# A gated mix of a long convolution and a token-shift MLP: keys and values channel by token instead of token by channel, and who does the small operations

## The chip, the cores and the metric

One core of one Trainium2 chip. The time is device microseconds of one launch, the median over runs; the profile is one further execution, recorded by the hardware profiler. Both kernels compute the same function in bf16 with sums in float32.

## The reference, cut to what matters

S is 2048 tokens, D 640 channels, F 1536.

```
k_shift[s] = sum over t in 0..3 of k[s - 3 + t] * shift_k[:, 3 - t]   # zeros ahead of the first token
kv  = k_shift * v
y   = irfft(rfft(kv padded to 2S) * rfft(ssm_k padded to 2S))[:S] + kv * ssm_D
a   = q * y
h   = gelu(layernorm(q) @ w1)                 # four channel groups, shifted by +1, -1, +2, -2 tokens
x1  = q + shifted(h) @ w2
b   = x1 + gelu(layernorm(x1) @ w3) @ w4
g   = sigmoid(sum over channels of q * gate_w)
out = g * a + (1 - g) * b
```

So there is a causal convolution of every channel of kv over all 2048 tokens with a filter of its own, and an MLP of two layers, mixed by one gate for each token.

## The kernel before, in words

**How order comes about.** The program is first recorded: `P.op` and `P.dma` note each operation with the memory it reads and writes, and from the memory follow the dependencies. A literal list SEQUENCE then gives the order in which the recorded operations are issued, and PLACES the PSUM bank of each matmul result; each engine gets its operations in that order and the semaphores between engines are put in where a dependency crosses. An engine never overtakes: whatever stands behind a waiting instruction in its list waits too. All SBUF tiles lie in one array (`arena`) and all PSUM tiles in another (`PSall`), so the profile tells them apart by shape and line only. Helpers hold the lines: `tt` (L636, two operands), `ts` (L641, one operand and scalars), `act` (L646, ACT), `mm` (L656, matmuls), `P.dma` (L238 plain, L235 as a DMA transpose).

**The convolution.** It is done blockwise in the frequency domain. Tokens are cut into 4 blocks of 512; a block's transform has 1024 points, of which the symmetries leave four groups `j` of 128 frequencies with a real and an imaginary part. A block is first *folded*: sums and differences of its halves, one of them reversed in time, so that each group of frequencies needs a matmul against only 128 or 256 rows. HF holds the filter's spectrum, XF that of kv, both as 2 halves of 320 channels x 4 blocks x (4 groups x 2 parts x 320).

- `h_load`, `h_fold`, `h_chunk` (L729 to 764), for each of 5 chunks of 128 channels: the filter lies channel by token, 128 x 2048. ACT reverses (4 x 255), two DVE operations of 1024 make the sum and the difference, two DMA transposes of 256 KB bring tokens onto the partitions, then 20 matmuls of 512 columns and four to eight evictions.
- `kv_half`, `kv_block` (L768 to 800), for each half of the channels g, block b and half block: k is loaded token by channel, 128 partitions x 5 neighbouring tokens x 320 channels (400 KB; the overlap serves the shift), v as 2 x 320 (160 KB). One DVE product of 2560 multiplies the 4 taps at once against the table SHK, in which the tap weights stand on all partitions; sums of 1280 and 640 add the taps; a product of 640 multiplies with v. A matmul with `flip` reverses one half block in time, ACT evicts it, and four DVE operations of 640 fold the block. For the first block a memset (L778) and three small loads stand in for the tokens ahead of the first.
- `x_fwd` (L802): 12 matmuls of 320 columns and four evictions of 640 for each g and b.
- `combine` (sums and differences of neighbouring blocks' spectra), `unit` (products of the spectra, 2560 wide, with accumulating DMAs issued by POOL for some of the sums), `final` (inverse transform, product with q, output).

**The MLP.** `ln_bn`/`bn_math`/`ln1`, `mm1` (whose token shifts are the operations of L891), `mmg` and `gate`, `mm2`, `ln2` with `ln_math`, `mm3`, `mm4`. Their statistics of 128 x 1 go over POOL (GpSimd) in good part: the power of -1/2 (`pool_pow`, L828) always, and small products and sums by the argument `eng="pool"`. POOL also issues the accumulating DMAs.

**Where it lies in time.** The MLP's first layer, the filter, the keys and values and the forward transforms share the first 119 us or so, `unit` and the MLP's second layer follow, and the inverse ends it.

Of the kernel before, what the change touches and what calls it, by code (L numbers as in the profile page):

```python
# [382 lines left out]
def _folded_dft():  # L383
# [5 lines left out]
    k = np.concatenate([np.arange(0, 256, 2), np.arange(1, 256, 2)])[None, :]  # L389
    ko = np.arange(256)[None, :]  # L390
    n = 2. * np.arange(128)[:, None] + .5
    m = 256 - n
    R = np.concatenate([np.cos(w * 2 * k * n), -np.sin(w * np.where(k == 0, 512, 2 * k) * n),
                        np.cos(w * (2 * ko + 1) * n), -np.cos(w * (2 * ko + 1) * m),
                        -np.sin(w * (2 * ko + 1) * n), -np.sin(w * (2 * ko + 1) * m)], 1)
    p = np.arange(128)[:, None]
    no = np.stack([p, p + 128])
    ne = np.where(no == 0, 256, no)
    Rh = np.stack([np.cos(w * 2 * k * ne),
                   np.where(k == 0, no == 0, -np.sin(w * 2 * k * no)),  # L400
                   np.cos(w * (2 * ko + 1) * no),
                   -np.sin(w * (2 * ko + 1) * ne)])
    Z = np.zeros((3, 128, 128))
    Z[:2, :, 0] = ((-1.) ** ne)[:, :, 0]
    Z[2, 0] = 1.
# [6 lines left out]
    Rh = Rh.transpose(2, 0, 1, 3)  # L412
    G = G.reshape(2, 2, 2, 128, 256).transpose(3, 0, 2, 1, 4)
    return (R, np.concatenate([Rh.reshape(128, 2048), Z.transpose(1, 0, 2).reshape(128, 384)], 1),
            G.reshape(128, 8 * 256))


def bass_gated_mix__ssm_conv_h3__mixer_s_mlp__prompt_kernel(
# [11 lines left out]
    cE = nc.inline_tensor(_bits(np.repeat(np.eye(5), 128, axis=1)), name="cE")  # L430

# [20 lines left out]
    def ps(n, cls):  # L452
# [3 lines left out]
    SEQUENCE = [57, 10, 31, 58, 28, 9, 11, 5, 56, 1, 27, 4, 7, 12, 0, 2, 59, 29, 13, 141, 30, 14, 63, 26, 35, 15, 64,  # L456
# [74 lines left out]

    HW = S + 4
    oXF = alloc(20480)
# [618 lines left out]
```

## Time and profile before

| | |
|---|---|
| runs | median 239.17 us, 237.65 to 246.24, 3 runs |
| profiled execution | span 236.6 us |
| matmuls of 320 columns, of 512 columns (L656) | 824, 390 |
| DVE instructions, POOL instructions | 402, 122 |
| moved by DMA | 45.48 MB in 63785 packets |

Engines in the profile: PE the matmuls, PEld their weight loads (beside PE), DVE the vector engine, ACT the scalar engine, POOL GpSimd, SP the engine that issues most DMAs. A group of instructions reads: line, engine, operation, output and input shape (partitions x elements), count, then busy time in us and the mean ns of one, then idle time of the engine just before them and what ended it. A row of waits reads: who waited, for what, total us, times, longest.

### The profile page before, as it was taken

To read this page: it belongs to the slowest core of one execution; us is meant where nothing else is said; L and a number is where in the kernel's file an instruction comes from. 1 tells how busy PE (TensorE), PEld (TensorE's weight loads), DVE (VectorE), ACT (ScalarE), POOL (GpSimd) and SP (SyncE) were. 2 spreads that over 40 slices of the span, in tenths; PEclk is the share of its full clock that TensorE was granted. 3 is DMA by queue.
4 is the path that set the end of the run, shared out by engine and by line. 5 is a ranking of instruction groups with operands and counts; after the bars stand their busy time and mean duration, and the time that the engine had idled before them with its cause. 6 is when DMAs were issued, how large, how long until landed. Compare 5 with 4: busy or idle time off the path is not lost.

```text
span 236.6 us, 4135 instructions
## 1 busy us (share of the span) xinstructions
PE 222.6 (94%) x1501; PEld 134.7 (57%) x1501; DVE 220.1 (93%) x402; ACT 171.2 (72%) x317; POOL 108.4 (46%) x122
## 2 busy tenths in 40 slices
PE   7999999999899999998989999899999999999861
PEld 2688755456444556444755457555677545776640
DVE  6889999899898789998899999999999999999975
ACT  2699889687588858998477763778968479258962
POOL 0330405810796008056109994564315256266960
PEclk9999999999999999999999999999999999999996
DMA  6999699996889999799527928869899978999996
GB/s 172 334 355 326 123 259 235 278 244 130 188 143 196 236 259 235 181 361 212 150 60 125 157 37 212 141 105 209 204 316 210 200 124 136 185 157 108 113 155 122
DMA packets 63785, 45.48 MB, mean 192 GB/s; under 512 B 28818, under 2 KB 59028, under 8 KB 63764
## 3 DMA queue, kind: packets, MB, share of 16 engines
q1 hardware_dynamic: 54748, 33.33, 56.5%
q0 software_dynamic: 8832, 11.80, 33.5%
q8 instruction: 12, 0.20, 0.3%
q10 hardware_dynamic: 184, 0.08, 0.1%
q14 instruction: 9, 0.07, 0.1%
HBM read 24.22 MB, written 6.55 MB: 130 GB/s over the span
## 4 chain that ended last, share of the span: by engine, by line
PE 30%; DMA 23%; DVE 20%; POOL 12%; issue 6%; SPq 4%; ACT 3%; DVEq 0%; POOLq 0%; ACTq 0%
PE PSall L656 27%; DVE arena L636 14%; DMA arena<-arena 8%; DMA arena<-in_A_v_dram 8%; DMA out_dram<-arena 6%; POOL out_dram L238 4%; ACT arena L646 3%; POOL arena L641 3%; PE PSall L682 3%; SPq L238 2%; POOL arena L828 2%; SPq L235 2%; DVE arena L641 2%; DVE arena L891 2%; DVE arena L824 1%
## 5 line engine op out<-in xcount | busy, mean ns | idle before, releaser
L656 PE MATMUL PSall<-arena 128*128 128x320 bf16 (+5 forms) x1444 | 214.9, 308 | 8.7 <-DVE arena L636 4.9
L636 DVE TENSOR_TENSOR arena<-arena 128x640 bf16<-128x640 bf16 (+5 forms) x247 | 183.0, 792 | 6.3 <-DMA arena<-in_A_v_dram 2.6
L656 PEld LDWEIGHTS PSall<-arena 128*128 128x128 bf16 (+1 forms) x1444 | 130.6, 98 | 92.0 <-DVE arena L636 7.4
L646 ACT ACTIVATE arena<-PSall 128x640 bf16<-128x640 f32 (+6 forms) x189 | 109.1, 632 | 34.9 <-PE PSall L656 33.5
L641 POOL TENSOR_SCALAR arena<-arena 128x1 f32<-128x1 f32 (+2 forms) x41 | 32.9, 811 | 44.2 <-DVE arena L825 22.6
L646 ACT ACTIVATE arena<-arena 128x640 bf16<-128x640 bf16 (+4 forms) x62 | 42.2, 701 | 6.9 <-POOL arena L636 3.8
L828 POOL TENSOR_TENSOR arena<-arena 128x1 f32<-128x1 f32 (+1 forms) x26 | 26.1, 1009 | 27.1 <-DVE arena L641 26.5
L238 POOL DMA_DIRECT2D out_dram<-arena x28 | 31.5, 1304 | 11.9 <-ACT arena L646 9.2
L238 POOL DMA_DIRECT2D arena<-arena x12 | 15.6, 1303 | 38.8 <-DVE arena L636 38.6
L646 ACT ACTIVATE arena<-PSall,arena 128x640 bf16<-128x640 f32 (+1 forms) x32 | 20.5, 658 | 17.6 <-PE PSall L656 16.1
L641 DVE TENSOR_SCALAR arena<-arena 128x640 bf16<-128x640 bf16 (+2 forms) x49 | 14.4, 306 | 2.9 <-DMA arena<-arena 1.4
L824 DVE BATCH_NORM_STATS2 arena<-arena 128x6 f32<-128x320 bf16 x32 | 14.2, 476 | 1.5 <-DMA arena<-in_A_q_dram 1.5
L682 PE MATMUL PSall<-arena 128*128 128x512 bf16 x15 | 6.1, 593 | 1.6 <-DVE arena L678 1.6
L636 POOL TENSOR_TENSOR arena<-arena 128x1 f32<-128x1 f32 (+1 forms) x11 | 7.2, 658 | 0.6
L926 DVE SCALAR_TENSOR_TENSOR arena<-PSall,arena 128x640 bf16<-128x640 f32 x8 | 6.5, 818 | 0.2 <-PE PSall L656 0.2
L891 DVE TENSOR_SCALAR arena<-arena 32x256 bf16<-32x256 bf16 (+1 forms) x24 | 5.7, 243 | 0.8 <-ACT arena L646 0.4
L646 ACT ACTIVATE PSall<-PSall 128x640 f32<-128x640 f32 x8 | 5.6, 701 | 0.1
L682 PEld LDWEIGHTS PSall<-arena 128*128 128x128 bf16 x15 | 2.0, 142 | 5.1 <-issue 3.5
L870 PE MATMUL PSall<-arena 128*128 128x128 bf16 x40 | 3.4, 220 | 0.0
L685 ACT ACT_TABLE_LOAD x1 | 1.3, 1283 | 2.7 <-issue 2.7
L825 DVE BATCH_NORM_AGGREGATE arena<-arena 128x2 f32<-128x12 f32 x16 | 3.0, 195 | 0.0
L870 PEld LDWEIGHTS PSall<-arena 128*128 128x128 bf16 x40 | 2.4, 98 | 0.7 <-DVE arena L825 0.2
(24 smaller groups left out, 9.3 us busy)
## 6 DMA issues: line engine op xcount, KB each, us to landing
arena<-arena POOLq DMA_DIRECT2D x12, 640.0 KB, 6.2
arena<-in_A_k_dram SPq DMA_DIRECT2D x14, 400.0 KB, 4.6
arena<-in_A_q_dram SPq DMA_DIRECT2D x14, 320.0 KB, 5.8
out_dram<-arena POOLq DMA_DIRECT2D x20, 160.0 KB, 4.9
arena<-in_A_ssm_k_dram SPq DMA_DIRECT2D x5, 512.0 KB, 6.0
arena<-in_A_v_dram SPq DMA_DIRECT2D x16, 160.0 KB, 4.3
arena<-in_B_w_dram SPq DMA_DIRECT2D x1, 1920.0 KB, 9.9
out_dram<-arena SPq DMA_DIRECT2D x10, 160.0 KB, 4.4
```

What stands on the lines that cost most here:

```text
L235: fn = lambda e: e.dma_start_transpose(out, in_)
L238: fn = lambda e: e.dma_start(out, in_, **kw)
L636: P.op(eng, lambda e: e.tensor_tensor(o, real(a), real(b), op), [a, b], [o], dve_ns(o, [a, b], 2) if eng == "dve" else 500)
L641: P.op(eng, lambda e: e.tensor_scalar(o, real(a), s1, s2, op0=op0, **({} if op1 is None else {"op1": op1})), [a] + aps, [o], dve_ns(o, [a] ...
L646: P.op("act", lambda e: e.activation(real(o), real(a), f, bias=bias, scale=scale, **({"accum_out": accum} if accum is not None else {})), ...
L656: fns.append(lambda e, l=l, r=r, i=i: e.matmul(real(o), l, r, start=(i == 0), stop=(i == last)))
L682: P.op("pe", lambda e: e.matmul(real(pw), warm[:, 0:128], warm[:, 128:640], start=True, stop=True), [warm], [pw], 427.0 if i < 14 else 216.0)
L824: P.op("dve", lambda e, o=o, i=i: e.bn_stats(o, i), [i], [o], 400)
L828: P.op("pool", lambda g: g.tensor_tensor(o, a, e, ALU.pow), [a, e], [o], dur)
L870: P.op("pe", [lambda e, c=c, pb=pb, xn=xn: e.transpose(real(pb)[:, 128 * c:128 * (c + 1)], xn[:, 128 * c:128 * (c + 1)], ident) for c in r ...
L891: P.op("dve", lambda e, o=hT[q, 4, c0:c0 + n], i=hx[q, :]: e.tensor_scalar(o, i, 1.0, None, op0=ALU.mult), [hx[q, :]], [hT[q, 4, c0:c0 + n ...
L926: P.op("dve", lambda e: e.scalar_tensor_tensor(x, real(pr), 1.0, x, op0=ALU.mult, op1=ALU.add, accum_out=st[1, 0][:, t:t + 1]), [pr, x], [ ...
```

## The change

- **Keys and values** are loaded by DMA transposes straight out of DRAM: 128 channels x 2048 tokens, 512 KB each, one of k and one of v for each of 5 chunks (`kv_load`). The shift by a token is then an offset along the row: `kv_taps` makes four operations of one operand with a weight for each channel (`taps`), three sums and one product with v, all 2048 wide. `kv_fold` does both folds in this layout (four DVE operations of 1024 and one reversal of 1024 on ACT), then one transpose of 512 KB (16 x 128) brings the folded tokens onto the partitions. `x_chunk` transforms with 12 matmuls of 512.
- **The filter** goes the same way: `h_fold` makes both folds ahead of one transpose of 512 KB, `spectrum` (shared by both) then needs 16 matmuls of 512 for a chunk in place of 20. The tables of cosines and sines follow.
- **The tap weights** are no table on all partitions any more but 20 columns, made by tiny matmuls.
- **POOL** keeps the powers and the accumulating DMAs; the other small operations (`bn_math`, `ln_math`, `gate`, `ln2`) go to DVE, with `ln_math` written in another way.
- **Memory**: chunk 0 of the keys has buffers of its own for v, products, folds and transposed blocks; chunks 1 to 4 share one set (`kv_at`), k alternates between two. `unit` takes its buffers from the same region.
- **SEQUENCE and PLACES** are new throughout. The chunks of keys stand in the order 1, 0, 2, 3, 4.

Counts that change (before, after): matmuls of 320 columns 824, 712; of 512 columns 410, 445 with the warm-up; DVE products of 2560 68, 52; sums of 1280 44, 28; operations of 640 with two operands 80, 16; of 1024 10, 40; of 2048 none, 40 (20 with one operand); DMA transposes 34, 44; POOL operations 52 fewer.

The diff, cut to its core:

```diff
@@ memory @@
+    kT = [V(oS + 2064 * i, 2064) for i in range(2)]
+    kv_at = [oXF + 10240, oS + 4128, oS + 4128, oS + 4128, oS + 4128]
+    h_at = [oXF, oXF + 5120, oXF, oXF + 5120, oXF]
-    ubuf = [V(o, 2560) for o in (oYX, oPT, oPT + 2560, oHT + 7680, oKV + 5120)]
+    ubuf = [V(oS + 2560 * i, 2560) for i in range(5)]
@@ filter @@
     def h_fold(c):
-        act(kr[:, :, 1:256], k[:, :, 511:256:-1], ACTF.Copy)
-        tt(fo[:, 1], k[:, :, 0:256], kr, ALU.subtract)
-        tt(fo[:, 0], k[:, :, 0:256], kr, ALU.add)
-        ts(fo[:, 0, :, 0:1], k[:, :, 256:257], 1.0, None, ALU.mult)
-        for e in range(2):
-            P.dma(sp, het[c % 2][:, e].rearrange("p b k c -> p (b k) c"), fo[:, e].rearrange("p b n -> p (b n)"), transpose=True)
+        tt(pm[:, 0], k[:, :, 0:256], k[:, :, 256:512], ALU.add)
+        tt(pm[:, 1], k[:, :, 0:256], k[:, :, 256:512], ALU.subtract)
+        act(rev[:, :, :, 0].rearrange("p m b -> p b m"), k[:, :, 256::-256], ACTF.Copy)
+        act(rev[:, :, :, 1:128], pm[:, :, :, 255:128:-1], ACTF.Copy)
+        tt(sd[:, 0], pm[:, :, :, 0:128], rev, ALU.add)
+        tt(sd[:, 1], pm[:, :, :, 0:128], rev, ALU.subtract)
...
+        P.dma(sp, ft, V(h_at[c], 2048), transpose=True)
@@ keys and values @@
-        tt(kpr, win, SHK[:, :, ds].unsqueeze(1).to_broadcast([128, 2, 4, 320]), ALU.mult)
-        tt(kpr[:, :, 0:2], kpr[:, :, 0:2], kpr[:, :, 2:4], ALU.add)
-        tt(kpr[:, :, 0], kpr[:, :, 0], kpr[:, :, 1], ALU.add)
-        tt(dst, kpr[:, :, 0], vt, ALU.mult)
+    def kv_load(c):
+        cs = slice(128 * c, 128 * (c + 1))
+        P.dma(sp, kT[c % 2][:, 16:2064].unsqueeze(1), A_k[0, :, cs], transpose=True)
+        P.dma(sp, V(kv_at[c], 2048).unsqueeze(1), A_v[0, :, cs], transpose=True)
+    def kv_taps(c):
+        k, v = kT[c % 2], V(kv_at[c], 2048)
+        t = [V(kv_at[c] + 2048 * (i + 1), 2048) for i in range(3)]
+        def tap(o, j):
+            w = taps[:, 5 * j + c:5 * j + c + 1]
...
+                ts(o, k[:, 16 - j:2064 - j], w, None, ALU.mult)
+        tap(t[0], 0)
+        tap(t[1], 1)
+        tt(t[0], t[0], t[1], ALU.add)
+        tap(t[2], 2)
+        tap(t[1], 3)
+        tt(t[1], t[1], t[2], ALU.add)
+        tt(t[0], t[0], t[1], ALU.add)
+        tt(t[0], t[0], v, ALU.mult)
+    def kv_fold(c):
...
+        tt(pm[:, 0], kv[:, :, 0:256], kv[:, :, 256:512], ALU.add)
+        tt(pm[:, 1], kv[:, :, 0:256], kv[:, :, 256:512], ALU.subtract)
+        act(rev, pm[:, :, :, 255:127:-1], ACTF.Copy)
+        tt(sd[:, 0], pm[:, :, :, 0:128], rev, ALU.add)
+        tt(sd[:, 1], pm[:, :, :, 0:128], rev, ALU.subtract)
+        P.dma(sp, V(kv_at[c] + 6144, 2048).rearrange("p (q c) -> p q c", q=16), V(kv_at[c] + 2048, 2048), transpose=True)
@@ small operations @@
-        ts(s[2], s[0], -1.0 / D, None, ALU.mult, eng="pool")
-        ts(s[4], s[2], s[2], 1e-5, ALU.mult, ALU.subtract, eng="pool")
-        ts(s[3], s[1], s[4], None, ALU.subtract)
+        ts(s[4], s[0], s[0], -1.0 / D / D, ALU.mult, ALU.mult)
+        ts(s[3], s[4], s[1], 1e-5, ALU.add, ALU.add)
+        ts(s[2], s[0], -1.0 / D, None, ALU.mult)
         pool_pow(s[5], s[3], neghalf[:, t:t + 1])
-        tt(off, mean, rstd, ALU.mult, eng="pool")
+        tt(off, mean, rstd, ALU.mult)
```

The order of the vector engine before, about one half block of keys and its neighbours (L636 is `tt`; 128x2560 the product with the four taps, 128x2x640 and the 128x2x320 behind it the sums of the taps and the product with v, 128x1280 sums of `combine`):

```order
L636 TENSOR_TENSOR arena<-arena 128x2560
L636 TENSOR_TENSOR arena<-arena 128x2x640
L636 TENSOR_TENSOR arena<-arena 128x1280
L636 TENSOR_TENSOR arena<-arena 128x2x320 x2
L636 TENSOR_TENSOR arena<-arena 128x2560
L636 TENSOR_TENSOR arena<-arena 128x2x640
L636 TENSOR_TENSOR arena<-arena 128x2x320
L778 MEMSET arena 32x480
```

In the change the vector engine's list reads as follows from the folds of chunk 3 to the taps of chunk 4 (`tt` is now L616, `ts` L621; 128x1024 the folds, the 128x2048 of L621 the taps, 128x1280 sums of `combine`, 128x1 the small statistics):

```order
L616 TENSOR_TENSOR arena<-arena 128x1280 x2
L616 TENSOR_TENSOR arena<-arena 128x1024 x2
L616 TENSOR_TENSOR arena<-arena 128x1
L621 TENSOR_SCALAR arena<-arena 128x2048
L616 TENSOR_TENSOR arena<-arena 128x1280
L621 TENSOR_SCALAR arena<-arena 128x1
L616 TENSOR_TENSOR arena<-arena 128x1
L621 TENSOR_SCALAR arena<-arena 128x2048
L616 TENSOR_TENSOR arena<-arena 128x2048
L621 TENSOR_SCALAR arena<-arena 128x2048
```

The last two folds of chunk 3 come right ahead of chunk 4: one tap (into a buffer that the folds have left free), a sum of `combine` and small operations stand between them and the second tap, which writes into the buffer that the transpose of chunk 3's folds reads. In the old order each half block had buffers in turn and no transpose.

The queue of SP in the change, about the last chunks (L235 are DMA transposes; those named in_A_k_dram and in_A_v_dram are the loads of `kv_load`, 128x16x128 the folded chunks 2 and 3, 128x5x128 those of the MLP):

```order
L235 DMA_TRANSPOSE arena<-in_A_k_dram 128x1x2048
L238 DMA out_dram<-arena 128x320
L235 DMA_TRANSPOSE arena<-in_A_v_dram 128x1x2048
L235 DMA_TRANSPOSE arena<-arena 128x16x128
L235 DMA_TRANSPOSE arena<-arena 128x5x128
L238 DMA out_dram<-arena 128x640 x2
L238 DMA arena<-cG 128x2048
L235 DMA_TRANSPOSE arena<-arena 128x5x128
L238 DMA arena<-in_B_w_dram 128x12x640
L235 DMA_TRANSPOSE arena<-in_A_v_dram 128x1x2048
```

The load of v for chunk 3 stands just ahead of the transpose of chunk 2's folds, and that for chunk 4 seven entries later; before, plain loads of k and v stood in their place among the MLP's transposes.

More of the change, by code (lines that the diff above doesn't have):

```diff
@@ L601, in small @@
         _s[0] += n
-        assert _s[0] <= 388
+        assert _s[0] <= 420
         return sm[:, o:o + n]
@@ L610, in bass_gated_mix__ssm_conv_h3__mixer_s_mlp__prompt_kernel @@
     gsum = small(2)
-    bfs = V(oSm + 776, 208)
+    taps = small(20)
+    bfs = V(oSm + 840, 200)
     dgT = bfs[:, 32:42]
@@ L1089, in bass_gated_mix__ssm_conv_h3__mixer_s_mlp__prompt_kernel, with xc, hc, cb @@
         at(ln2, t)
-    for g in range(2):
-        for b in (3, 2, 1, 0):
-            at(kv_block, g, b)
-            at(x_fwd, g, b)
+    def xc(c):
+        for f in (kv_load, kv_taps, kv_fold, x_chunk):
+            at(f, c)
+    def hc(c):
+        for f in (h_load, h_fold, h_chunk):
+            at(f, c)
+    def cb(g):
         for b in (3, 2, 1):
             at(combine, g, b)
+    for c in range(5):
+        hc(c)
+    for c in range(5):
+        xc(c)
+        if c % 2 == 0 and c:
+            cb(c // 2 - 1)
     at(w4_load)
```

239 lines of the change are left out of this document (95 added, 144 removed), and 141 rows, old and new, of tables (PLACES, SEQUENCE).

## The prediction

> **What bounds the kernel now.** I read the page's busy times first, then the busy times by stretches of the span, then the waits, then the groups of instructions by shape, which carry the prices.
>
> ```profile
> span 236.6 us, 4135 instructions
> PE 222.6 (94%) x1501; PEld 134.7 (57%) x1501; DVE 220.1 (93%) x402; ACT 171.2 (72%) x317; POOL 108.4 (46%) x122
> ```
>
> Two engines are nearly full, PE and DVE; ACT and POOL are not. An average says nothing of where the idle time lies, so the same in two halves. At 119.2 us DVE starts the products of the two spectra (`unit`), and all but the last few forward folds are behind it. The columns are PE, PEld, DVE, ACT, POOL busy, the granted clock, the DMA share and GB/s.
>
> ```profile
> 0.00:119.20 119.20, 113.95 (x815) 68.18 (x815) 107.76 (x257) 92.07 (x177) 44.31 (x67) 1.00 0.94 229
> 119.20:200.00 80.80, 79.79 (x482) 46.87 (x483) 80.45 (x80) 57.23 (x101) 43.43 (x37) 1.00 0.80 161
> 119.20:236.60 117.40, 108.62 (x686) 66.51 (x686) 112.37 (x146) 79.18 (x141) 64.10 (x55) 0.98 0.87 155
> ```
>
> From 119.2 to 200 both engines have no gap at all (80.45 and 79.79 of 80.8), so what comes after the start of `unit` lasts as long as DVE's list there, and that list is not edited (52 products of 2560, their combinations and the `final` steps). In the first half DVE has 11.4 us of idle time, PE 5.3. So the time is set by when DVE gets through its first half: its own work there, and its waits. The waits of DVE over the whole span (total, times, longest), those that the sum needs:
>
> ```profile
> DVE arena L636 <- DMA arena<-in_A_v_dram: 2.6, 3, 1.3
> ...
> DVE arena L641 <- PE PSall L656: 0.8, 1, 0.8
> DVE arena L641 <- POOL arena L828: 0.8, 1, 0.8
> ...
> DVE arena L641 <- PE PSall L870: 0.5, 1, 0.5
> DVE arena L891 <- ACT arena L646: 0.4, 1, 0.4
> ```
>
> They are many and small; the largest single cause is the loads of v, 2.6 us. DVE waits once for POOL, 0.8 us: its slow small operations hold up little.
>
> **The change, part by part.** The prices come from these rows (busy time divided by the count, or the mean of one):
>
> ```profile
> L636 DVE TENSOR_TENSOR arena<-arena 128x2560 bf16<-128x2560 bf16 x68 | 98.7, 1483 | 0.8 <-DVE arena L636 0.6
> L636 DVE TENSOR_TENSOR arena<-arena 128x1280 bf16<-128x1280 bf16 x44 | 35.3, 816 | 0.3
> L636 DVE TENSOR_TENSOR arena<-arena 128x640 bf16<-128x640 bf16 x80 | 37.4, 484 | 3.2 <-DMA arena<-in_A_v_dram 2.6
> L636 DVE TENSOR_TENSOR arena<-arena 128x1024 bf16<-128x1024 bf16 x10 | 6.7, 667 | 0.0
> L641 DVE TENSOR_SCALAR arena<-arena 128x640 bf16<-128x640 bf16 x24 | 10.4, 436 | 2.7 <-DMA arena<-arena 1.4 <-POOL arena L828 0.8 <-PE PSall L870 0.5
> L641 DVE TENSOR_SCALAR arena<-arena 128x1 f32<-128x1 f32 x20 | 3.7, 187 | 0.1
> L891 DVE TENSOR_SCALAR arena<-arena 32x256 bf16<-32x256 bf16 x16 | 3.5, 220 | 0.3
> L891 DVE TENSOR_SCALAR arena<-arena 32x512 bf16<-32x512 bf16 x8 | 2.3, 287 | 0.5 <-ACT arena L646 0.4
> L824 DVE BATCH_NORM_STATS2 arena<-arena 128x6 f32<-128x320 bf16 x32 | 14.2, 476 | 1.5 <-DMA arena<-in_A_q_dram 1.5
> L926 DVE SCALAR_TENSOR_TENSOR arena<-PSall,arena 128x640 bf16<-128x640 f32 x8 | 6.5, 818 | 0.2 <-PE PSall L656 0.2
> L636 DVE TENSOR_TENSOR arena<-arena 128x1 bf16<-128x1 bf16 x5 | 0.7, 138 | 0.0
> L778 DVE MEMSET arena<- 32x480 uint32 x2 | 0.9, 458 | 0.1
> ```
>
> *DVE, keys and values.* Gone are 16 products of 2560 (16 x 1.451 = 23.2), 16 sums of 1280 (16 x 0.802 = 12.8), 64 operations of 640 (64 x 0.468 = 29.9) and the two memsets (0.9): 66.8 us. Added for five chunks are 20 taps, 20 two-operand steps of 2048 and 20 of 1024. The two-operand slope is (1.451 - 0.802)/1280 = 0.507 ns an element, so 2048 costs 0.802 + 768 x 0.507 = 1.19 us, and 20 are 23.8; 20 of 1024 at 0.67 are 13.4. A tap has no row: its slope is that of L891, (287 - 220)/256 = 0.26 ns, its fixed part that of the 640-wide scalar operation, 0.433 + 1408 x 0.26 = 0.80 us, 20 are 16.0. Sum 53.2, so this part saves 13.6 us.
>
> *DVE, the filter.* 20 operations of 1024 in place of 10 and five tiny ones: +6.7 + 0.7 = 7.4 us. Together with the keys DVE saves 6.2 us.
>
> *DVE, the small operations that leave POOL.* 41 scalar operations and 11 two-operand ones go to DVE: by busy time 41 x 0.185 + 11 x 0.14 = 9.1 us. Recorded times of neighbours overlap (the 2560-wide products have a mean of 1483 ns, and busy time by count gives 1451, 32 ns counted twice). At the cheapest row less that overlap they cost 52 x (0.138 - 0.032) = 5.5. So DVE's work changes by -0.7 to +2.9 us. I take +1.2, about the middle. All of it is in the first half, where DVE sets the pace, so it counts in full.
>
> *PE.* 112 matmuls of 320 columns go (96 forward, 16 reversals), 60 of 512 come with the new forward transform, 20 of the filter's and the 5 of the taps go.
>
> ```profile
> L656 PE MATMUL PSall<-arena 128*128 128x320 bf16 x824 | 120.5, 299 | 6.8 <-DVE arena L636 4.9 <-ACT arena L646 1.2 <-DVE arena L926 0.4
> L656 PE MATMUL PSall<-arena 128*128 128x512 bf16 x390 | 90.9, 379 | 1.4 <-DMA arena<-arena 1.1 <-ACT arena L646 0.2
> L656 PE MATMUL PSall<-arena 5*128 5x512 bf16 x5 | 1.9, 382 | 0.0
> ```
>
> -112 x 0.146 + 40 x 0.233 - 1.9 = -9.0 us, all in the first half. That is much for PE, but it ends nothing by itself: DVE, at 221.3 us, is now the fuller of the two by 8 us. Its worth is that DVE waits less for PE.
>
> *ACT and POOL.* ACT loses 40 evictions of 640 (27.7 us) and five of 512 (2.8), and gains 16 of 1024 (16.1), 8 of 512 (4.5) and five reversals (5.3): about -5 us. POOL loses 52 operations that DVE takes over.
>
> ```profile
> L646 ACT ACTIVATE arena<-PSall 128x640 bf16<-128x640 f32 x64 | 44.3, 701 | 16.2 <-PE PSall L656 15.6
> L646 ACT ACTIVATE arena<-PSall 128x1024 bf16<-128x1024 f32 x16 | 16.1, 1026 | 3.6 <-PE PSall L656 3.4
> ```
>
> Neither sets the end now, so I give both nothing, except that DVE's waits for PE, ACT and POOL (0.8 + 0.5, 0.8 and 0.4) may go: -2.5 us at best, and 0 at worst if the statistics that DVE now reads from ACT put the same waits back. I take -2.5, since all three engines lose work. The loads of v are waited for no more (-2.6): the first transposes of k and v wait for nothing and stand behind 22 loads on SP, 22 x 0.58 = 13 us by the row of k's issues, while the first tap stands behind 31 of the 32 statistics and the folds of two filter chunks, 31 x 0.44 + 8 x 0.67 = 19 us.
>
> ```profile
> L238 SPq DMA_DIRECT2D arena<-in_A_k_dram x20: 374/582/833, 7.5 to 112.4; - x20
> arena<-in_A_k_dram SPq DMA_DIRECT2D x14, 400.0 KB, 4.6
> ```
>
> *The new wait.* Chunks 1 to 4 share one set of buffers for v, products, folds and transposed blocks. So the tap of chunk 4 that writes the first of them stands on DVE behind the transpose that reads chunk 3's fold, and a later tap behind the twelve matmuls that read that transpose's output. Everything on DVE is queued behind the waiting tap, PE's transform of chunk 4 and `unit` of the first half of the channels above all. How long is a transpose?
>
> ```profile
> L235 SPq DMA_TRANSPOSE arena<-arena x34: 1207/1278/2687, 23.3 to 174.1; - x34
> DMA to landing us min/median/max: 2.6/3.9/5.6
> DMA packets 1950, 0.50 MB, mean 249 GB/s; under 512 B 1926, under 2 KB 1950, under 8 KB 1950
> ```
>
> Those are of 160 and 256 KB; the third row is a stretch of 2 us (64 to 66 us) with hardly anything but transposes, 0.50 MB. The new ones have 512 KB: by that rate 352 KB more take 1.4 us, so 4.0 us at the least from issue to landing, 5.3 at the median, 7.0 at the longest. Between the last fold of chunk 3 and the waiting tap stand only a tap, a combination and a few tiny operations, 0.80 + 0.80 + 0.3 = 1.9 us: the wait is 2.1 to 5.1 us, I take 3.4. For chunk 3 three PSUM additions of 0.82 us lie between as well, 3.8 us in all: 0.2 to 3.2, hidden if PE is in time, and I take 0.2. Chunk 2 has some ten us of other work there: nothing. The twelve matmuls, 12 x 0.233 = 2.8 us, run beside 2.8 us of taps: 0 to 2.8, I take 0.3.
>
> *DMA queues.* SP issues 36 loads of k and v fewer (some 0.58 us each) and 10 transposes more (1.28): its queue gets shorter by 8 us. The bytes that the transposes move rise from 24 x 160 + 10 x 256 KB to 24 x 160 + 20 x 512 KB, 6.6 to 14.4 MB; the loads of k and v, some 9 MB, go. With a DMA share of 0.94 in the first half this is the part that I know least.
>
> **The sum**, against the profile's own span: 236.6 + 1.2 (DVE's work) - 2.6 (v) - 2.5 (other waits) + 3.4 + 0.2 + 0.3 (the shared buffers) = 236.6 us. The median of the runs, 239.17, lies 2.6 us above the profiled span; so 239.2 us.
>
> **A rule that speaks against it.** Two of the four taps read the keys at an odd element, so 10 of 20 start off a 4-byte boundary. No row shows an odd start on the reading side; on the writing side L891 writes half its 24 results at odd elements:
>
> ```profile
> L891 DVE TENSOR_SCALAR arena<-arena x24: 216/222/290, 17.2 to 76.8; 32x256 bf16<-32x256 bf16 x16, 32x512 bf16<-32x512 bf16 x8
> ```
>
> The 16 of 256 columns all lie at 216 to 224 ns, odd or even. If a tap lost its rate all the same, at the two-operand slope it would cost 2048 x (0.507 - 0.26) = 0.5 us more, 5 us for ten, 244.2 us in all. The Trainium skill, in "VectorE: DVE Perf Modes", section "Mode 2×_1P — pack two bf16 into one 32-bit read", asks for a 4-byte aligned start for that mode and, through it, for the fourfold one; in "Vector Engine (DVE) Microarchitecture Reference", section "5.1 Performance modes — why throughput varies by op and dtype", it says that alignment makes no difference. The trace sides with the second as far as it goes.
>
> **The rivals.**
>
> *Faster: PE was the bound after all, and DVE's gaps were its echo.* For it: in the first half PE is busy 113.95 of 119.2, more than DVE. Against it: after 119.2 DVE is as full, and it starts the half late by its own 11.4 us. If PE's 9.0 us come through whole, the span is 227.6. DVE has room for that: beside its 221.3 us it keeps only the gaps at the start and the end, which no order can fill,
>
> ```profile
> 0.93 0.59 DVE L678 MEMSET arena<- 128x640 bf16 x1 [0.93 <-PEq L1139]
> ...
> 3.05 1.28 DVE L824 BATCH_NORM_STATS2 arena<-arena 128x6 f32<-128x320 bf16 x3 [0.91 <-DMA arena<-in_A_q_dram]
> ...
> 228.95 5.24 DVE L636 TENSOR_TENSOR arena<-arena 128x320 bf16<-128x320 bf16 x17 [1.35 <-DMA out_dram<-arena]
> ```
>
> 0.9 + 0.9 + 1.4 and the 2.4 us behind its last result: 226.9. Between all of it and half of it, 227.6 to 232.1, with the 2.6: 230 to 235, middle 232.5 us.
>
> *Slower: the shared buffers.* If the 512 KB transposes land 8.5 us after their issue rather than 5.3, because v's transpose of the next chunk and the accumulating transfers stand on the same engines (share 0.94), chunk 3 pays 4.7 us, chunk 4 6.6 and its later tap 2.8, 14.1 in place of 3.9: 249.4 us. It decides the sign from a landing of about 5.3 us on, the value taken, and passes 2% at about 7.
>
> *Slower: transposes out of DRAM.* No row has one. At the SBUF rate each takes 2.1 us of all queues; a 400 KB load of k, 640 rows, lands in 4.6 us, so 2048 rows priced like k's rows would take 2 + 2.6 x 3.2 = 10 us, and the folds queued behind v3 and v4 would come 6 us later each: 251 us.
>
> **How the numbers follow.** Forecast as summed: 0.44. PE's share comes through: 0.29. Shared buffers wait long: 0.15. Slow DRAM transposes: 0.08. Odd taps: 0.04. With every term of the sum at its lower end the forecast is 235.5, with every one at its upper end 250.6, which four would have to reach together. The range for 8 in 10 takes in most of the faster case and the nearer part of the slower ones: 231 to 248. Two per cent, 4.8 us, is about what a measurement of this kernel tells from no change: the forecast lies well within it; the last three cases are slower, the second faster.
>
> **What would show it.** Right: DVE busy near 221 us and PE near 214; DVE full from the first 2560-wide product to the end, with that product starting near 120 us; a gap of 2 to 5 us on DVE ahead of a 2048-wide scalar operation just before it, ended by a transpose. Taps of 0.7 to 0.8 us, all four alike. Wrong: PE's idle time staying at 14 us while the span falls by 8 (PE was the bound); taps of two lengths; transposes of k and v that land after 8 us or more; several DVE gaps of more than 5 us at the chunks' changes.

## The result and the profile after

The changed kernel takes 245.32 us (median of 4 runs, 244.26 to 247.76), the kernel before 238.41 us beside it; the ratio is 1.032, 95% interval 1.024 to 1.040. One of the four executions of the kernel before ran in a slower state of the chip (246.24 us); the median above counts it, the ratio here and below leaves such executions out. The change is slower by some 7 us, inside the range of 231 to 248, but 6 us above the forecast of 239.2 us. The profiled execution spans 242.5 us against 236.6: 5.9 us to explain.

The first lines of the page of the changed kernel answer to those of before (DVE 220.1 of 236.6, PE 222.6):

```profile
span 242.5 us, 3885 instructions
PE 217.8 (90%) x1428; PEld 126.5 (52%) x1428; DVE 218.5 (90%) x431; ACT 171.2 (71%) x307; POOL 66.5 (27%) x70
```

DVE and PE both do less, and the program takes longer. So the time went into waits. Adding up the trace's idle stretches of DVE from its first instruction to its last gives 13.1 us before and 19.7 us after, +6.6; its work is 1.6 us shorter, and 3.3 us follow its last result where 2.4 did, +0.9. Together 5.9. The loss lies in the first half: the first product of `unit` starts at 127.3 us where it started at 119.2 (forecast: near 120), and from there to the end the changed kernel takes 115.2 us where 117.4 stood.

Which waits? The waits of DVE by what ended them (total, times, longest), first the row of the kernel before for transfers inside SBUF, then those of the changed kernel:

```profile
DVE arena L641 <- DMA arena<-arena: 1.4, 3, 0.8
```

```profile
DVE arena L621 <- DMA arena<-arena: 5.8, 4, 2.8
DVE arena L621 <- ACT arena L626: 3.9, 4, 2.8
DVE arena L616 <- DMA arena<-arena: 2.5, 2, 2.2
...
DVE arena L621 <- PE PSall L636: 0.8, 2, 0.4
DVE arena L900 <- PE PSall L636: 0.7, 1, 0.7
DVE arena L616 <- POOL arena L802: 0.7, 1, 0.7
```

The waits for v are gone, as forecast. But waits for transfers inside SBUF rose from 1.4 to 8.3 us, those for ACT from 0.6 to 4.1. Transfers inside SBUF are transposes but for the twelve accumulating ones of `unit`; all but 0.3 us of the 8.3 is for transposes. Three places show these waits. The first, on SP's queue (start, length, issue):

```profile
58.03 2.83 SPq L235 DMA_TRANSPOSE arena<-in_A_k_dram  x1
60.90 1.28 SPq L235 DMA_TRANSPOSE arena<-arena  x1
62.23 0.58 SPq L238 DMA_DIRECT2D arena<-in_A_ssm_k_dram  x1
62.85 6.98 SPq L235 DMA_TRANSPOSE arena<-arena  x3
```

A load of k holds SP for 2.83 us. Behind it stands the layer norm's small transpose of 60.90, which lands after 4.63 us at 65.5, and DVE, which wants to write the buffer that this transpose reads, waits 2.76 us for it, until 65.56. The second place goes by way of ACT:

```profile
90.59 0.74 ACT L626 ACTIVATE arena<-arena 128x640 bf16<-128x640 bf16 x1 [2.52 <-DMA arena<-arena]
...
91.45 0.21 DVE L621 TENSOR_SCALAR arena<-arena 128x1 f32<-128x1 f32 x1 [2.77 <-ACT arena L626]
```

ACT uses one of the layer norm's two buffers as scratch, waits 2.52 us for the transpose that still reads it, and DVE, whose list now holds the small statistic, waits 2.77 us for ACT. This transpose is issued at 85.59 us, ahead of the next load of k (87.46) and not behind one; it lands after 4.97 us, where the one issued at 83.72 took 2.62. That landing, 2.35 us longer, makes the wait, and no load of k ahead of it in the queue; why it lands so late is not shown. The third place is the one the prediction spoke of, chunk 4's taps and then `unit`:

```profile
117.67 0.75 DVE L621 TENSOR_SCALAR arena<-arena 128x2048 bf16<-128x2048 bf16 x1 [1.79 <-DMA arena<-arena]
...
120.95 0.87 DVE L621 TENSOR_SCALAR arena<-arena 128x1 f32<-128x1 f32 x2 [0.48 <-ACT arena L626]
...
123.49 0.21 DVE L621 TENSOR_SCALAR arena<-arena 128x1 f32<-128x1 f32 x1 [0.41 <-ACT arena L626]
...
135.31 2.90 DVE L616 TENSOR_TENSOR arena<-arena 128x2560 bf16<-128x2560 bf16 x2 [2.24 <-DMA arena<-arena]
```

The second tap waits 1.79 us for chunk 3's transpose (forecast 3.4), which lands 4.55 us after its issue (forecast 5.3), and a product of `unit` 2.24 us for chunk 4's, in a buffer that overlaps it: that wait was in no term of the sum.

Three prices, for the account at the end:

```profile
L616 DVE TENSOR_TENSOR arena<-arena 128x2048 bf16<-128x2048 bf16 x20 | 24.4, 1221 | 0.2
L621 DVE TENSOR_SCALAR arena<-arena 128x2048 bf16<-128x2048 bf16 x20 | 14.8, 745 | 3.4 <-DMA arena<-arena 2.6 <-PE PSall L636 0.8
L621 DVE TENSOR_SCALAR arena<-arena 128x1 f32<-128x1 f32 x52 | 8.3, 183 | 4.0 <-ACT arena L626 3.9
```

### The profile page after: what moved, and what is told of

The parts are those of the page before. It is cut to its first block, busy times and chain, and to the rows that moved or that the text cites. A ratio compares the mean times of both kernels' runs of the same rounds, so it can differ in the third digit from the quotient of the medians.

```text
span 242.5 us, 3885 instructions
## 1 busy us (share of the span) xinstructions
PE 217.8 (90%) x1428; PEld 126.5 (52%) x1428; DVE 218.5 (90%) x431; ACT 171.2 (71%) x307; POOL 66.5 (27%) x70
## 4 chain that ended last, share of the span: by engine, by line
DVE 56%; DMA 20%; ACT 9%; issue 6%; PE 4%; POOL 2%; SPq 2%; POOLq 0%; DVEq 0%
DVE arena L616 45%; DMA arena<-arena 13%; ACT arena L626 9%; DVE arena L621 6%; PE PSall L636 4%; DMA out_dram<-arena 4%; DMA arena<-in_A_ssm_k_dram 3%; DVE arena L798 3%; DVE arena L865 2%; SPq L238 2%; POOL out_dram L238 1%; POOL arena L238 0%; DVE arena L799 0%; DVE arena L900 0%; DVE arena L682 0%
## 5 line engine op out<-in xcount | busy, mean ns | idle before, releaser
L636 PE MATMUL PSall<-arena 128*128 128x320 bf16 (+4 forms) x1367 | 209.4, 310 | 17.5 <-ACT arena L626 6.6
L636 PEld LDWEIGHTS PSall<-arena 128*128 128x128 bf16 x1367 | 122.0, 98 | 104.1 <-ACT arena L626 17.2
L616 DVE TENSOR_TENSOR arena<-arena 128x2560 bf16<-128x2560 bf16 (+9 forms) x217 | 162.6, 807 | 6.0 <-DMA arena<-arena 2.5
L626 ACT ACTIVATE arena<-PSall 128x512 bf16<-128x512 f32 (+7 forms) x169 | 102.3, 652 | 30.0 <-PE PSall L636 24.8
L626 ACT ACTIVATE arena<-arena 128x640 bf16<-128x640 bf16 (+6 forms) x72 | 49.1, 705 | 15.7 <-DVE arena L616 11.3
L802 POOL TENSOR_TENSOR arena<-arena 128x1 f32<-128x1 f32 (+1 forms) x26 | 23.1, 919 | 98.6 <-DVE arena L621 98.6
L621 DVE TENSOR_SCALAR arena<-arena 128x1 f32<-128x1 f32 (+5 forms) x110 | 33.5, 339 | 10.6 <-DMA arena<-arena 5.8
L238 POOL DMA_DIRECT2D out_dram<-arena x28 | 29.4, 1320 | 44.6 <-ACT arena L626 39.1
L238 POOL DMA_DIRECT2D arena<-arena x12 | 14.5, 1205 | 27.4 <-DVE arena L616 25.2
L662 PEld LDWEIGHTS PSall<-arena 128*128 128x128 bf16 x15 | 2.0, 139 | 4.9 <-issue 3.0
L844 PEld LDWEIGHTS PSall<-arena 128*128 128x128 bf16 x40 | 2.4, 98 | 1.3 <-DVE arena L621 1.1
L626 ACT ACTIVATION_READ_ACCUMULATOR arena<-arena 128x1 f32 x8 | 1.8, 221 | 0.0
L626 ACT ACTIVATION_READ_ACCUMULATOR arena<-PSall 128x1 f32 x8 | 1.6, 194 | 0.0
```

What stands on the lines that cost most here:

```text
L238: fn = lambda e: e.dma_start(out, in_, **kw)
L616: P.op(eng, lambda e: e.tensor_tensor(o, real(a), real(b), op), [a, b], [o], dve_ns(o, [a, b], 2) if eng == "dve" else 500)
L621: P.op(eng, lambda e: e.tensor_scalar(o, real(a), s1, s2, op0=op0, **({} if op1 is None else {"op1": op1})), [a] + aps, [o], n_of(o) / 3.8 ...
L626: P.op("act", lambda e: e.activation(real(o), real(a), f, bias=bias, scale=scale, **({"accum_out": accum} if accum is not None else {})), ...
L636: fns.append(lambda e, l=l, r=r, i=i: e.matmul(real(o), l, r, start=(i == 0), stop=(i == last)))
L662: P.op("pe", lambda e: e.matmul(real(pw), warm[:, 0:128], warm[:, 128:640], start=True, stop=True), [warm], [pw], 427.0 if i < 14 else 216.0)
```

## The experiments

Times are medians; each ratio is to the kernel before on the same chip, with its 95% interval. The intervals reach 0.3 to 0.8% to either side, so a difference of less than about 2.5 us between two versions is not settled by their times. By that measure `e_own`, `e_plain`, `e_pool`, `e_join` and `e_lightpe` cannot be told from the changed kernel, `e_xn4` and `e_join_act` lie at the edge, and the differences of `e_late`, `e_all`, `e_xn4_few` and `e_j2_few` are clear. The first four runs change one thing in the changed kernel.

**Chunk 4 with buffers of its own** (`e_own`).

```diff
+    t_at = [[kv_at[c] + 2048 * (i + 1) for i in range(3)] for c in range(5)]
+    t_at[4] = [oS + 2080, kv_at[4] + 4096, oHT + 7680]
+    sd_at = [kv_at[c] + 2048 for c in range(4)] + [oS]
-    ubuf = [V(oS + 2560 * i, 2560) for i in range(5)]
+    ubuf = [V(oS + 2560 * i, 2560) for i in (1, 2, 3, 0, 4)]
```

In `kv_taps` and `kv_fold` the buffers come from `t_at` and `sd_at`, and in SEQUENCE the table of the inverse transform stands behind chunk 4's transpose.

> Chunk 4 of the keys gets buffers of its own for the first tap, the third tap and the folded tokens, and the products of the spectra take their buffers in an order that starts with free ones; the table of the inverse transform is loaded later. In the changed kernel DVE stands 1.79 us at 117.7 us and 2.24 us at 135.3 us for the transposes of chunks 3 and 4. Theory A (the shared buffers cost what DVE waits there): both gaps go, 4.0 us, so 241.3 us and 1.013 of the kernel before. Theory B (the waits of the first half are links of one chain, and whoever is freed waits for the next): the gaps go, others grow, at most 1 us is gained, 244 us or more.

Measured: 244.53 us, 1.028 (1.025 to 1.032), 0.8 us less than the changed kernel. The gap at the tap is gone, and this stands in its place:

```profile
121.19 0.88 DVE L624 TENSOR_SCALAR arena<-arena 128x1 f32<-128x1 f32 x2 [1.09 <-ACT arena L629]
124.18 0.21 DVE L624 TENSOR_SCALAR arena<-arena 128x1 f32<-128x1 f32 x1 [0.85 <-ACT arena L629]
136.25 1.49 DVE L619 TENSOR_TENSOR arena<-arena 128x2560 bf16<-128x2560 bf16 x1 [0.95 <-DMA arena<-arena]
139.07 5.17 DVE L619 TENSOR_TENSOR arena<-arena 128x2560 bf16<-128x2560 bf16 x6 [1.33 <-PE PSall L639]
145.29 3.63 DVE L619 TENSOR_TENSOR arena<-arena 128x2560 bf16<-128x2560 bf16 x3 [1.06 <-DMA arena<-arena]
```

DVE comes to the next two statistics of ACT and waits for them (1.94 us in place of 0.89), then three times in `unit` (3.3 us in place of 2.2). The sizes are rough: in this execution DVE reached chunk 4's first tap 1.5 us later than in the changed kernel (114.60 us against 113.09). The time is that of theory B: the shared buffers are waited for, and taking the wait away is worth little.

**Four buffers for the layer norm's result** (`e_xn4`).

```diff
-    xn2 = [V(oXN + 640 * i, 640) for i in range(2)]
+    xn2 = [V(o + 640 * i, 640) for o in (oXN, oS + 12800) for i in range(2)]
```

Both uses of it take `t % 4` in place of `t % 2`.

> The MLP's second layer norm gets four buffers in place of two between its result and the transpose that reads it. In the changed kernel DVE stands 2.76 us at 65.6 us for such a transpose that is issued behind a load of k, and 2.77 us at 91.5 us for statistics of ACT, which itself stood 2.52 us for such a transpose. Theory A (late transposes cost what DVE waits for them): both go, up to 5.5 us, 240 to 241 us. Theory B (one chain of waits): less than 1.5 us gained, 244 us or more, and the idle time of DVE ahead of 127 us stays near 16 us.

Measured: 242.46 us, 1.021 (1.014 to 1.028). Both gaps are gone, and 2.9 us of their 5.5 are gained. Other waits grew in their place: 2.03 us for a chunk's transpose at 98.6 us where 0.77 stood, 2.3 us in all for the filter's loads where 0.4 stood, and a new one of 1.2 us for ACT. About midway between the two theories.

**The small operations back on POOL** (`e_pool`). The edit puts `eng="pool"` back on the small operations that had left POOL, 52 by the instruction counts (POOL 70 to 122, DVE 431 to 379) and not the 49 of the expectation.

> Of the operations that left POOL, 49 go back to it (two of each layer norm's three, the second shift, the gate, the variance of later tokens). Theory A (they cost DVE their own time, some 0.1 us each where one starts after the other): 49 x 0.11 = 5.4 us less work on DVE, 240 to 241 us. Theory B (POOL's latency, 0.8 us an operation, comes back into the chain of the statistics for which DVE waits): what is saved is waited for, 244 to 247 us.

Measured: 246.37 us, 1.037 (1.029 to 1.045): not faster.

```profile
PE 216.8 (89%) x1414; PEld 126.5 (52%) x1428; DVE 214.6 (88%) x379; ACT 171.4 (70%) x307; POOL 89.4 (37%) x122
```

DVE does 3.9 us less and is idle 5.5 us more (25.2 in all). Theory B in time: what is saved is waited for. But only 2.3 us of the new waits are for POOL; the waits for transfers inside SBUF grew from 8.3 to 11.1 us and those for the filter's loads from 0.4 to 1.8. That POOL's latency (0.9 us for one such operation in the kernel before) also delays what those transposes need is likely, and not shown.

**Plain loads in place of the transposes out of DRAM** (`e_plain`).

```diff
-        P.dma(sp, kT[c % 2][:, 16:2064].unsqueeze(1), A_k[0, :, cs], transpose=True)
-        P.dma(sp, V(kv_at[c], 2048).unsqueeze(1), A_v[0, :, cs], transpose=True)
+        flat = lambda a: bass.AP(a.tensor, a.offset + 128 * c * S, [[S, 128], [1, S]])
+        P.dma(sp, kT[c % 2][:, 16:2064], flat(A_k))
+        P.dma(sp, V(kv_at[c], 2048), flat(A_v))
```

> The ten transposes out of DRAM become plain loads of as many bytes into the same buffers, so that keys and values are not those of the reference; everything else stands. Theory A (the transposes out of DRAM hold SP for 2 to 3 us each and delay the transposes behind them): SP is free some 17 us earlier in sum, the gap of 2.76 us at 65.6 us goes and the landings of the others get shorter, 3 to 5 us, 240 to 242 us. Theory B (they are hidden, the waits come from the buffers and the order): 244 us or more.

Measured: 243.22 us, 1.023 (1.016 to 1.031), 2.1 us less. The gap at 65.6 us is gone. SP's issues ahead of 120 us add up to 92.3 us, 14 us less than in the changed kernel (106.4), while the waits for the folded chunks 3 and 4 stay (2.02 and 2.25 us). Between the theories again: with plain loads SP's issues took much less time, and more than half of the loss stayed, as did the layer norm's two buffers.

The next four ask what sets the pace at all.

**The three kinds of wait taken on together** (`e_join`): `e_xn4` and `e_own` together, with `sd_at[2] = oXF + 10240`.

> The four buffers of the layer norm and chunk 4's own buffers together, and the folded tokens of chunk 2 where chunk 0 had its products, so that chunk 3's first tap finds its buffer free too. With the four buffers alone DVE still stood 2.03, 2.16 and 2.22 us at 98.6, 117.0 and 133.5 us for transposes of shared buffers; chunk 4's own buffers alone gained 0.8 us, since statistics of ACT were waited for in their place. Theory A (two kinds of late transpose, each hiding the other): the join gains more than the sum of both, 6.4 us beyond the four buffers at best, 236 to 239 us and a ratio of 0.99 to 1.005. Theory B (after each wait stands the next): 241 us or more, ratio 1.01 or more.

Measured: 244.06 us, 1.027 (1.018 to 1.035), so 1.3 us gained in all, no more than by the four buffers alone. One reason is at 68 us. First SP, then DVE:

```profile
58.76 2.96 SPq L235 DMA_TRANSPOSE arena<-in_A_k_dram  x1
61.77 1.28 SPq L235 DMA_TRANSPOSE arena<-arena  x1
63.09 0.58 SPq L238 DMA_DIRECT2D arena<-in_A_ssm_k_dram  x1
```

```profile
68.21 1.49 DVE L619 TENSOR_TENSOR arena<-arena 128x1 bf16<-128x1 bf16 x4 [2.94 <-DMA arena<-in_A_ssm_k_dram]
```

DVE is not held by the layer norm any more, and stands 2.94 us for the filter's last load, which is issued two places behind the same load of k. In `e_xn4` DVE came to the same load 1.7 us later and waited 0.46 us. So here DVE stands for a plain load, not for a transpose, that is late in SP's queue. Theory A of this run, that each wait hid the other and both could be had, fell.

**One tap on ACT** (`e_join_act`): `TAP_ACT = {2}` in `e_join`.

> As e_join, and the third of the four taps of each chunk is made by ACT: five operations of 2048 leave DVE, 5 x 0.67 = 3.3 us, and ACT gets five of some 1.9 us. Theory A (DVE's work sets the pace once its waits are gone): 2 to 3 us faster than e_join. Theory B (waits between the engines set it): no faster than e_join, or slower, since a sum on DVE waits for ACT.

Measured: 247.31 us, 1.043 (1.036 to 1.049). DVE's busy time falls from 218.3 to 215.2 us, and its sums wait for ACT's tap instead:

```profile
DVE arena L619 <- ACT arena L629: 10.9, 4, 3.5
```

**PE with less to do** (`e_lightpe`).

```diff
-for i, q in enumerate((0, 3) if r else (2, 1))]
+for i, q in list(enumerate((0, 3) if r else (2, 1)))[:1]]
```

> The changed kernel with one of the two matmuls left out in each of the odd groups of both forward transforms, 40 of 512 columns in ten chunks, so that its spectra are not those of the reference: 40 x 0.233 = 9.3 us less on PE, nearly all ahead of 127 us. Theory A (in that half DVE's work and its waits for transposes set the pace): less than 2 us gained. Rival (PE is the bound): 7 to 9 us gained, 236 to 238 us.

Measured: 243.31 us, 1.024 (1.019 to 1.029), 2.0 us less for 5.9 us less of PE's busy time (211.9; 9.3 less was expected). The rival, 7 to 9 us, is out: PE's work is not what sets the time of the changed kernel. The gain just reaches theory A's limit of 2 us.

**The small operations alone, in the kernel before** (`b_small`): every `eng="pool"` of the kernel before is dropped.

> The kernel before, with the small operations moved from POOL to DVE, and nothing else: that part of the change alone. Theory A (each costs DVE 0.11 us, and its waits stay): 52 x 0.11 = 5.6 us, 243 to 245 us, ratio 1.02 to 1.03. Theory B (POOL's latency sat in the chain of the statistics and its end gives back what DVE loses): 237 to 240 us, ratio 0.995 to 1.01.

Measured: 241.77 us, 1.017 (1.011 to 1.023): +4.0 us.

```profile
span 239.2 us, 4131 instructions
PE 222.6 (93%) x1501; PEld 134.5 (56%) x1501; DVE 223.8 (94%) x454; ACT 171.1 (72%) x317; POOL 73.5 (31%) x70
```

DVE has 3.7 us more to do (0.07 us for each of 52), its idle time is 12.1 us where 13.1 stood, and the time grows by what DVE's work grows. So in the kernel before DVE's work does set the pace. The time lies between the two ranges; the way is that of theory A, at two thirds of its price.

Then SP's queue itself.

**Four transposes out of DRAM issued later** (`e_late`). In SEQUENCE k of chunk 2 stands behind the fold of filter chunk 3, v of chunk 2 behind that of filter chunk 4, k of chunk 3 behind one and k of chunk 4 behind another of the layer norm's transposes.

> The changed kernel with four of the ten transposes out of DRAM moved back on SP (k and v of chunk 2, k of chunks 3 and 4): between 17 and 75 us SP issues one after the other, and these four, 8.5 us of issue ahead of 61 us, are needed only 10 to 40 us later, while the layer norm's transposes and the filter's last loads behind them are waited for (2.76 us at 65.6 us; in e_join 2.94 us for the filter at 68.2 us). Theory A (SP's queue, full of transposes, delays what DVE needs next): the gaps between 60 and 70 us go, 2 to 3.5 us gained, 241.8 to 243.3 us. Theory B (DVE meets the next wait at the same time as before): less than 1 us gained.

Measured: 250.52 us, 1.055 (1.048 to 1.061): 5 us slower. The gaps at 65 to 68 us did go. SP and DVE of this kernel behind that place:

```profile
66.88 7.10 SPq L235 DMA_TRANSPOSE arena<-arena  x4
74.02 2.74 SPq L235 DMA_TRANSPOSE arena<-in_A_v_dram  x1
76.80 1.28 SPq L235 DMA_TRANSPOSE arena<-arena  x1
78.12 2.31 SPq L235 DMA_TRANSPOSE arena<-in_A_k_dram  x1
```

```profile
72.73 1.86 DVE L621 TENSOR_SCALAR arena<-arena 128x2048 bf16<-128x2048 bf16 x4 [2.26 <-DMA arena<-arena]
79.55 0.45 DVE L621 TENSOR_SCALAR arena<-arena 128x640 bf16<-128x640 bf16 x1 [2.26 <-DMA arena<-arena]
...
86.15 0.45 DVE L621 TENSOR_SCALAR arena<-arena 128x640 bf16<-128x640 bf16 x1 [1.85 <-DMA arena<-arena]
```

The loads now stand among the transposes of the layer norm's next tokens, one of which DVE needs every few us. My theory that these loads only had to be moved out of the way was wrong: at that place there is no room for them either. That their place alone moves the time by 5 us supports the cause in another way: it matters what stands behind them in the queue.

**The same with all the buffers** (`e_all`): `e_late`, the four buffers, and own buffers for chunk 4's taps and chunk 2's folds, with `ubuf` as it was.

> The later transposes out of DRAM, the four buffers of the layer norm, and buffers of their own for chunk 4's first and third tap and chunk 2's folded tokens, all together; the products of the spectra keep their order of buffers. Theory A (late transposes of three kinds, of which each alone is hidden by the next, are what the change lost): 237 to 240 us, ratio 0.995 to 1.007. Theory B (the rest is a chain of small statistics between DVE, ACT and PE that no transpose sets): 241.5 us or more, ratio 1.013 or more, with DVE's waits for ACT grown.

Measured: 247.25 us, 1.044 (1.039 to 1.049). Theory A fell; the buffers gain 3.3 us of what the later loads lose.

**Six of the ten transposes out of DRAM nearly taken away** (`e_xn4_few`): in `e_xn4`, for chunks 2 to 4 a load of 64 columns in place of each.

> As e_xn4, and of the ten transposes out of DRAM the six of chunks 2, 3 and 4 are loads of 16 KB in place of 512 KB, so that the keys and values of these chunks are not those of the reference. It takes 3.1 MB and some 14 us of issue out of SP's queue between 46 and 111 us. Theory A (late transposes are what the change lost, and those out of DRAM delay the rest): 238 to 240 us, ratio 1.00 to 1.01, and the waits of DVE for transposes fall below 5 us from 7.4. Theory B (a chain through PE and ACT, whoever is freed): 241.5 to 243 us, no better than e_xn4 by more than 1 us.

Measured: 239.25 us, 1.006 (1.001 to 1.011), 3.2 us less than `e_xn4`, and within about 1% of the kernel before.

```profile
span 236.4 us, 3873 instructions
PE 215.4 (91%) x1414; PEld 126.5 (53%) x1428; DVE 218.2 (92%) x431; ACT 171.1 (72%) x307; POOL 66.4 (28%) x70
```

```profile
DVE arena L621 <- DMA arena<-arena: 3.1, 3, 2.1
DVE arena L616 <- DMA arena<-arena: 2.7, 2, 2.4
```

DVE's work is the changed kernel's (218.2), its idle time 13.4 us, that of the kernel before (13.1). Waits for transposes stay, 5.8 us, mostly the two at chunk 4 (2.11 and 2.41 us). Against `e_xn4` the wait for the folded chunk at 98.6 us fell from 2.03 to 0.58 us, those for the filter's loads from 2.3 to 0.7, and one of 1.2 us for ACT is gone. Theory A in time and ratio, not in its count of waits (below 5 us).

**And with the buffers of `e_all`** (`e_j2_few`).

> As e_xn4_few, and chunk 4's first and third tap and chunk 2's folded tokens have buffers of their own: of what DVE waited for transposes only the last chunk's stays. Theory A: 2 us or more below e_xn4_few, 236 to 238 us. Theory B: within 1 us of e_xn4_few, the idle time turned into waits for statistics of ACT and for PE.

Measured: 239.95 us, 1.013 (1.007 to 1.019), no faster than `e_xn4_few`. The waits for transposes fall to 4.6 us, and 2.5 us of waits for ACT's statistics come. Theory B, for the shared buffers a second time.

No version was faster than the kernel before.

## Why the prediction was right, and where it failed

The range held the time, the sign did not come out: the change is slower by 3%, which cases of mine with 0.27 covered, while the forecast with 0.44 saw no difference. That the range held it was partly luck: it was drawn wide for rivals that priced other mechanisms, and the loss came from a place that has no term in the sum.

- **DVE sets the pace of the kernel before: right.** 3.7 us more work on it cost 4.0 us (`b_small`), and the time rose although PE's busy time fell by 4.8 us.
- **DVE's work, forecast +1.2 us: measured -1.6.** The prices of the new operations held: 1.22 us for 2048 with two operands (1.19 forecast), 0.74 for a tap (0.80). The small operations were dearer on paper: 5.5 to 9.1 us forecast, 3.7 measured. So, if that price holds in the changed kernel too, the keys and the filter save 5.3 us (6.2 forecast), and the small operations take back 3.7.
- **The waits for v go, -2.6 us: right.**
- **"-2.5 us, since all three engines lose work": wrong.** DVE's waits for PE, ACT and POOL grew from 2.9 to 6.3 us. The reason given for them held only in part: POOL's busy time fell by 41.9 us, but PE's by 4.8 where 9.0 was forecast, and ACT's, forecast to fall by 5, is 171.2 us in both kernels. Besides, less work of an engine need not shorten a wait for one result of it: the statistics that DVE took over are computed between ACT's steps, and ACT waits in its turn for transposes (4.0 us, 2.52 of it in the second place above).
- **The shared buffers: place right, price beside the point.** 1.79 us at chunk 4 and 0.77 + 0.32 at chunk 3 stand against 3.4, 0.2 and 0.3, and 2.24 us in `unit` were missed. Taking such waits away gained 0.8 us in `e_own` and nothing in `e_j2_few`, neither clear of noise: other waits stood there in their place.
- **"its queue gets shorter by 8 us": the step that failed.** I priced the new transposes at 1.28 us of issue, the median of those of 160 and 256 KB. These are the rows of the changed kernel:

```profile
L235 SPq DMA_TRANSPOSE arena<-arena x34: 1199/1278/3608, 31.7 to 148.0; - x34
L235 SPq DMA_TRANSPOSE arena<-in_A_k_dram x5: 2286/3050/9036, 17.1 to 87.5; - x5
L235 SPq DMA_TRANSPOSE arena<-in_A_v_dram x5: 1428/2133/2710, 26.2 to 108.3; - x5
```

A transpose out of DRAM holds SP for 2.1 us (v) or 3.05 us (k) at the median, the first for 9.0, and those within SBUF up to 3.6. The 9.0 us belong to the place and not to DRAM: in `e_plain`, where a transpose within SBUF is the first behind the opening loads, that one holds SP for 10.25 us. Adding up all of SP's issues in the traces gives 104.3 us before and 120.9 after, 16.6 longer, not 8 shorter. The 36 loads that went had taken 24.3 us (20.9 forecast); the ten transposes out of DRAM take 31.7 and the 34 within SBUF 4.9 more than before, 36.7 together where the prediction had 12.8; other issues take 4.1 more. Of the issues that start ahead of 120 us alone the sums are 84.4 and 106.4, 22 us more. Between 20 and 60 us the share of the DMA engines is above one, so that packets overlap in the records, where 0.94 and 0.98 stood (columns as in the prediction; first the kernel before, then the changed one):

```profile
20.00:40.00 20.00, 20.00 (x163) 14.02 (x161) 19.39 (x50) 17.93 (x42) 5.01 (x10) 1.00 0.94 213
40.00:60.00 20.00, 19.05 (x126) 10.44 (x124) 18.40 (x42) 15.40 (x28) 7.35 (x10) 1.00 0.98 229
60.00:80.00 20.00, 19.17 (x119) 9.85 (x118) 18.38 (x44) 15.14 (x25) 14.26 (x18) 1.00 0.97 178
80.00:100.00 20.00, 19.42 (x116) 10.99 (x115) 17.81 (x35) 15.58 (x26) 4.98 (x8) 1.00 0.91 226
```

```profile
20.00:40.00 20.00, 18.33 (x157) 13.31 (x156) 19.67 (x72) 14.51 (x37) 4.77 (x7) 1.00 1.13 218
40.00:60.00 20.00, 17.79 (x125) 9.30 (x124) 19.38 (x48) 16.39 (x27) 5.36 (x7) 1.00 1.07 204
60.00:80.00 20.00, 18.32 (x93) 8.49 (x91) 17.09 (x43) 17.00 (x29) 0.00 (x0) 1.00 1.00 215
80.00:100.00 20.00, 17.61 (x97) 8.83 (x95) 15.05 (x41) 17.48 (x27) 2.40 (x3) 1.00 0.92 177
```

What stands behind these transposes is issued late: the layer norm's transpose at 60.9 us and the filter's last load in `e_join`. A folded chunk in `e_xn4` is issued only 0.5 us after its last fold (93.22 against 92.71), and lands after 5.4 us where it takes 4.4 in `e_xn4_few`. As a whole, once issued, the transposes within SBUF land no later than before (3.7 us at the median against 3.9, of those whose landing is on record). DVE's busy time falls to 17.1 and 15.1 us in the third and fourth stretch (18.4 and 17.8 before). With four buffers and without six of the ten, DVE's extra idle time is gone (`e_xn4_few`), with its work unchanged. That six of the ten transposes and the layer norm's two buffers together cost the time is shown by that run; that they do it through SP's queue is shown at single places only, and the second large wait, at 91 us, comes from a landing whose delay is not explained. I had called this "the part that I know least" and put no term on it.

- **The rivals.** PE as the bound: out, by `e_lightpe` and by its 4.8 us less work in a slower kernel. Slow transposes out of DRAM (0.08): the nearest. They land 4.1 to 5.6 us after their issue (the first one 12.6), not 10; what they cost, they seem to cost in the main by delaying what follows in SP's queue. Shared buffers (0.15): its waits were there, but not its price. Odd taps: 20 taps, ten of them with an odd start, have a mean of 745 ns, the shortest 697 and the longest 754. The Trainium skill's page "VectorE: DVE Perf Modes" (section "Mode 2×_1P — pack two bf16 into one 32-bit read") would have half of them slower; these rows do not show it and side with its "Vector Engine (DVE) Microarchitecture Reference", section "5.1 Performance modes — why throughput varies by op and dtype".

What stays open: whether it is SP's time to issue or the DMA engines' time to move 256-byte packets that holds the queue. `e_plain` relieves both, by 2.1 us in time, and `e_xn4_few` relieves both and takes 3.1 MB of transfers away; no run parts them. The issue times themselves do not: the 34 transposes within SBUF hold SP for 53.9 us in the changed kernel and 66.4 in `e_plain`, so an issue's length depends on what else is under way and is no fixed price. The four buffers were not run with all ten plain loads, nor the six small loads with two buffers. Nor was an order of instructions made for POOL's small operations in the changed kernel; `e_pool` used that made for DVE.

## What to carry to other kernels

When a change moves work from an engine to DMA transposes, price the queue that issues them with the larger transfer's own issue time, and list what stands behind each in that queue: here more was lost there than at the consumers of the transposes. In an order of instructions made ahead, a wait that is taken away uncovers the next, so that single waits read from a profile cannot be added up as gains: 5.5 us of waits were worth 2.9 here, and 4.0 were worth 0.8. What an engine's work is worth has to be measured in the kernel at hand: 3.7 us more on DVE cost 4.0 in the kernel before, and 3.9 us less gained nothing in the changed one, where POOL's latency came with it.

## What the runs showed of the hardware

A transpose of 512 KB out of DRAM occupied the issuing queue 1.3 to 4.5 us in these runs (the first one, behind the opening loads, 8.2 to 9.1, and a transpose within SBUF at that place 10.25), a plain load of as many bytes 0.43 us at the median (`e_plain`). 52 small operations on DVE, most of them 128 x 1 and recorded at 183 ns in the changed kernel, added 0.07 us each to its busy time in the kernel before (`b_small`). And a coincidence that I did not test: at 87.3 us in the changed kernel, at the second of the three places above, where a transpose of 160 KB took 4.97 us to land rather than 2.6, a fetch of instructions of 16 KB lies among its packets, and for about 1.5 us hardly any other packet moves. That the one delays the other is only a guess.
